# Chunked linear attention and an MLP on one core: later chunks' attention in 64x64 tiles, two halves of 64 times, one visit per group

## The chip, the cores and the metric

The kernel runs on one core of a Trainium2 chip. The metric is the device time of one execution in microseconds. The kernel before was timed three times: median 529.92 us (528.95, 529.92 and 985.7). One execution of it was profiled; its own time is 529.4 us, of which the profile's span, from the first instruction to the last, is 527.7 us.

Engines are named as in the profile: PE is TensorE (matmuls; PEld its weight loads), DVE VectorE, ACT ScalarE, POOL GpSimd, and SP the engine whose queue issues all DMAs here. PSUM is the memory that TensorE writes; the kernel uses it as eight banks of 512 f32 columns on 128 partitions.

## What is computed

Four sequences, eight heads, 768 times, 48 features a head. A linear attention with a decaying 48x48 state per sequence and head gives `y`; all heads' `y` of a time, 384 numbers, go through an MLP with an exact Gelu and 2048 hidden features.

```python
def _attn_ref(r, k, v, w, u):
    state = np.zeros((B, H, D, D), dtype=np.float32)
    for t in range(S):
        kt, vt, rt = (k[:, :, t], v[:, :, t], r[:, :, t])
        cur = np.einsum('bhd,bhe->bhde', u[None] * kt, vt)
        y[:, :, t] = np.einsum('bhd,bhde->bhe', rt, state + cur)
        state = w[None, :, :, None] * state + np.einsum('bhd,bhe->bhde', kt, vt)

def _moe_ref(x, w_in, w_out):
    h = x @ w_in
    g = 0.5 * h * (1.0 + erf(h * inv_sqrt2))
    return (g @ w_out).astype(np.float32)
```

## The kernel before

Time is cut into six chunks of 128 (`NCH`, `C`), heads into four pairs (`NP`). A *group* `gi` is one chunk of one pair, with all four sequences: 24 groups, `gi // 4` the chunk. Inside a chunk the attention is matrix products: the *scores* of all keys against all receptances of the chunk (L399), masked to the past (L406) with the bonus `u` on the diagonal (L375); the *new* part, the masked scores times the values (L425); the *old* part, the state at the chunk's start seen by the receptances (L419); and the *gain*, the chunk's own contribution to the state (L431), which L440 adds to the decayed state `Sbd`. Decays are put into the factors: L366 scales `r` and `k` by powers of `w` kept in `W`, and the keys of the gain are scaled by `WN` (L385). The result stands in the PSUM bank `Y`; L458 and L459 split it into a rounded high part and a remainder for the MLP, and 64 KB DMAs (L465) bring the fourth pair's features to where the other pairs leave gaps.

A pair lies on 112 partitions: one head on 0 to 47, the other on 64 to 111. The attention's products are plain f32, each of which leaves two records in the profile. The MLP's are in a rounded 32-bit format (`F32R`) and leave one record each, with every factor split into two parts, so that a step has three triples of matmuls into the hidden layer (L473, bank `Hp`) and three out of it (L513, banks `O`). A *step* is one chunk's 512 columns against 128 of the 2048 hidden features: 16 steps a chunk, 96 in all. Two Gelus (L501, L502) and a subtraction (L503) stand between.

The weights arrive as 64-bit numbers and are split on the chip, once, in the first 16 steps: three ScalarE and four VectorE operations a step (L304 to L316).

The first chunk's groups have their own forms (`plain`), with no state to look at. Groups of later chunks have the scores in 64x32 tiles, so as to leave out future times in blocks of 32, and their products are two separate entries of TensorE's list: scores and old part at one visit, new part and gain at another, with MLP triples between.

The order on every engine is worked out while the program is built, by `Plan.run`. Each operation is added with its engine, an estimated duration, a due time and the names it reads and writes. The planner walks through a simulated clock and gives each engine, of what is ready, the operation that is due first. `LATER` as due time means that an operation is due when its users need it. The engines then run their lists strictly in that order, so an operation whose input is late holds up all behind it on its engine. SP's DMAs are in such a list too. A group's loads go into one of two slots (`T`, `N`), by the parity of `gi`, and wait till the group two before has done with it.

`count_plain` checks that all decays lie in a range in which the chunked form is exact enough; outside it a slow general form follows, which isn't run with these inputs.

## Time and profile before

| | |
|---|---|
| median of 3 runs | 529.92 us |
| profiled execution | 529.4 us |
| its span | 527.7 us |
| PE busy | 510.1 us (97%) |
| DVE, ACT, POOL busy | 249.0, 219.7, 85.4 us |
| granted TensorE clock, mean | 0.977 |

The page shows busy times over the whole span, and the span in 40 slices of 13.2 us, in which a digit is a tenth of a slice:

```profile
PE   6899889999999999999999999999999999999995
PEld 4777667777887877778777878878787787888884
DVE  8979999996442433423433524334334213211111
ACT  2468778666424243334234343342442322322221
POOL 7650430312202202012022022011011000000000
PEclk8579999999999999999999999999999999999999
```

A group of records is given as line, engine, operation, what it writes and reads, its tile shape, the partitions and elements, and how many. A row of the timeline begins with the start and the length in microseconds. The length of a matmul's record is a model and runs on into the next one's, so what a block of matmuls costs is read from the start of one block to the start of the next.

### The profile page before, as it was taken

The page shows a single profiled execution, that of the slowest core. Times are in us where ns is not written, and L with a number is a line of the kernel's source. Part 1 is how long each engine was busy: PE and PEld are TensorE (multiplying, and loading weights), DVE is VectorE, ACT ScalarE, POOL GpSimd, SP SyncE. Part 2 cuts the span into 40 slices and gives each one's busy share as a digit, 9 for nine tenths or more (in the row PEclk, how much of TensorE's full clock was granted, in tenths as well). Part 3 has the DMA queues.
Part 4 walks back from the last instruction along what each step waited for, and adds up shares of the span by engine and source line. Part 5 has one row for each costly group of instructions (what it writes and reads, how often), then busy time and mean ns, then how long its engine had stood idle before and what let it go on. Part 6 is the DMA issues. An engine that isn't in the chain of part 4 may idle for free.

```text
span 527.7 us, 9445 instructions
## 1 busy us (share of the span) xinstructions
PE 510.1 (97%) x4039; PEld 406.3 (77%) x4039; DVE 249.0 (47%) x344; ACT 219.7 (42%) x467; POOL 85.4 (16%) x77
## 2 busy tenths in 40 slices
PE   6899889999999999999999999999999999999995
PEld 4777667777887877778777878878787787888884
DVE  8979999996442433423433524334334213211111
ACT  2468778666424243334234343342442322322221
POOL 7650430312202202012022022011011000000000
PEclk8579999999999999999999999999999999999999
DMA  8926665530330211411202403203313000100001
GB/s 242 362 70 202 214 181 179 203 91 32 111 89 2 91 50 43 140 34 58 91 1 90 142 0 91 63 29 91 101 40 91 1 11 11 60 1 1 1 0 65
DMA packets 13167, 44.51 MB, mean 84 GB/s; under 512 B 1792, under 2 KB 2176, under 8 KB 13120
## 3 DMA queue, kind: packets, MB, share of 16 engines
q1 hardware_dynamic: 13120, 43.86, 26.3%
q8 instruction: 33, 0.54, 0.4%
q14 instruction: 14, 0.11, 0.1%
HBM read 37.16 MB, written 4.72 MB: 79 GB/s over the span
## 4 chain that ended last, share of the span: by engine, by line
PE 77%; DVE 11%; DMA 4%; ACT 3%; issue 2%; POOL 2%; SPq 0%; DVEq 0%; POOLq 0%; ACTq 0%
PE Hp L473 32%; PE O L513 30%; PE Y L425 4%; PE A L399 4%; PE Y L419 3%; DMA Nb<-in_rkv_dram 3%; DVE wa L312 2%; DVE wa L310 1%; ACT Am L375 1%; DVE wl L316 1%; DMA raw<-in_wmlp_dram 1%; PE Y L513 1%; PE U L431 1%; DVE gl L503 1%; DVE Ts L343 1%
## 5 line engine op out<-in xcount | busy, mean ns | idle before, releaser
L473 PE MATMUL Hp<-xx,wh 128*128 128x512 f32 x576 | 169.3, 401 | 0.7 <-ACT gf L502 0.7
L503 DVE TENSOR_TENSOR gl<-gf,gh 128x512 fp32r<-128x512 f32 x95 | 75.8, 798 | 196.2 <-ACT gf L502 193.9
L473 PEld LDWEIGHTS Hp<-xx,wh 128*128 128x128 f32 x576 | 104.3, 188 | 25.3 <-ACT gf L502 2.4
L501 ACT ACTIVATE gh<-Hp 128x512 fp32r<-128x512 f32 x95 | 56.6, 595 | 151.6 <-PE Hp L473 151.6
L473 PE MATMUL Hp<-xx,wl 128*128 128x512 f32 x288 | 83.8, 398 | 1.2 <-DVE wl L316 1.2
L513 PE MATMUL O<-gh,wh 128*128 128x512 f32 (+1 forms) x285 | 81.6, 393 | 3.1 <-ACT gh L501 3.1
L513 PE MATMUL O<-gh,wl 128*128 128x512 f32 (+1 forms) x285 | 80.6, 390 | 0.0
L513 PE MATMUL O<-gl,wh 128*128 128x512 f32 (+1 forms) x285 | 80.4, 389 | 0.0
L361 POOL TENSOR_TENSOR Nb<-Nb 128x384 f32<-128x384 f32 x20 | 23.0, 1151 | 308.6 <-DMA Nb<-in_rkv_dram 293.0
L375 ACT ACTIVATE Am<-diag,cs 128x128 f32<-128x128 f32 x176 | 56.0, 392 | 28.3 <-DVE cs L368 28.2
L513 PEld LDWEIGHTS O<-gh,wh 128*128 128x128 f32 x285 | 52.6, 188 | 17.2 <-ACT gh L501 4.7
L473 PEld LDWEIGHTS Hp<-xx,wl 128*128 128x128 f32 x288 | 53.6, 188 | 15.8 <-DVE wl L316 2.8
L513 PEld LDWEIGHTS O<-gl,wh 128*128 128x128 f32 x285 | 52.7, 188 | 11.6
L513 PEld LDWEIGHTS O<-gh,wl 128*128 128x128 f32 x285 | 52.6, 188 | 11.7
L502 ACT ACTIVATE gf<-Hp 128x512 f32<-128x512 f32 x96 | 56.7, 591 | 0.0
L458 ACT CAST xx<-Y 112x512 fp32r<-112x512 f32 (+1 forms) x16 | 9.4, 588 | 69.5 <-PE Y L425 69.5
L406 DVE COPY_PREDICATED Am<-past,A 128x512 f32<-128x512 uint32 x44 | 29.6, 724 | 17.5 <-PE A L399 17.5
L440 DVE SCALAR_TENSOR_TENSOR Sbd<-Sbd,P,U 48x192 f32<-48x192 f32 x32 | 13.1, 411 | 29.0 <-PE U L431 28.5
L366 DVE TENSOR_TENSOR Tb<-Tb,W 112x1024 f32<-112x1024 f32 x20 | 25.2, 1262 | 2.7 <-DMA Tb<-in_rkT_dram 2.4
L363 POOL TENSOR_TENSOR Nb<-Nb,u_sb 128x384 f32<-128x384 f32 x20 | 24.2, 1211 | 1.5
L419 PE MATMUL Y<-Tb,Sbd 112*112 112x128 f32 x160 | 22.4, 283 | 0.0
L399 PEld LDWEIGHTS A<-Tb 48*32 48x32 f32 (+1 forms) x1280 | 16.7, 105 | 7.0 <-issue 6.6
(106 smaller groups left out, 396.9 us busy)
## 6 DMA issues: line engine op xcount, KB each, us to landing
raw<-in_wmlp_dram SPq DMA_DIRECT2D x16, 768.0 KB, 5.0
Nb<-in_rkv_dram SPq DMA_DIRECT2D x20, 576.0 KB, 4.6
Tb<-in_rkT_dram SPq DMA_DIRECT2D x20, 448.0 KB, 3.7
out_dram<-raw SPq DMA_DIRECT2D x5, 768.0 KB, 4.8
xx<-x SPq DMA_DIRECT2D x30, 64.0 KB, 3.1
T<-in_rkT_dram SPq DMA_DIRECT2D x4, 448.0 KB, 6.5
N<-in_rkv_dram SPq DMA_DIRECT2D x4, 384.0 KB, 9.0
out_dram<-raw SPq DMA_DIRECT2D x2, 256.0 KB, 2.5
```

The costliest lines, as they stand in the source:

```text
L361: add("pool", pool(DM), LATER, lambda: nc.gpsimd.tensor_tensor(out=n[:, 0], in0=n[:, 0], in1=n[:, 1], op=ALU.mult), r=[NK], w=[NR])
L363: add("pool", pool(DM), LATER, lambda: nc.gpsimd.tensor_tensor(out=n[:, 0], in0=n[:, 0], in1=u_sb[:, p, :].unsqueeze(1).to_broadcast([C, N ...
L366: add("dve", dve(1024), LATER, lambda: nc.vector.tensor_tensor(out=flat(t), in0=flat(t), in1=decay, op=ALU.mult), r=["P", f"W{p}"], w=[TR])
L375: add("act", 293, LATER, lambda j=j, b=b: nc.scalar.activation(out=am[:, j, b, :], in_=diag, func=AF.Copy, scale=sums[:, 2 * b + j:2 * b + ...
L399: nc.tensor.matmul(X[j][q, b * C + t0:(b + 1) * C], lhsT=t[l, 1, b, q], rhs=t[l, 0, b, t0:], start=True, stop=True)
L406: add("dve", 600, LATER, lambda j=j: nc.vector.copy_predicated(out=am[:, j], mask=past.bitcast(U32).unsqueeze(1).to_broadcast([C, NB, C]), ...
L419: nc.tensor.matmul(y[:LP, b * C:(b + 1) * C], lhsT=Sbd[:, p, b, :], rhs=t[:, 0, b, :], start=(b == 0), stop=False, skip_group_check=True)
L473: nc.tensor.matmul(Hp, lhsT=wt[j][:, 0, k_ * 128:(k_ + 1) * 128], rhs=x[:, a, k_, :], start=start and k_ == ks[0], stop=stop and k_ == ks[-1])
L501: add("act", 480, LATER, lambda: nc.scalar.activation(out=high, in_=Hp, func=AF.Gelu), r=["H"], w=[GH])
L502: add("act", 480, LATER, lambda: nc.scalar.activation(out=gf, in_=Hp, func=AF.Gelu), r=["H"], w=["gf"])
L503: add("dve", dve(512), LATER, lambda: nc.vector.tensor_tensor(out=low, in0=gf, in1=high.bitcast(F32), op=ALU.subtract), r=["gf", GH], w=[GL])
L513: nc.tensor.matmul(dst[:, a:b], lhsT=wt[j][:, 1, d * 128:(d + 1) * 128], rhs=gt[:, a:b], start=(j == 0 and n == 0), stop=(j == NJ - 1 and ...
```

## The change

Groups of the first chunk are as before (`first_group`). For later chunks, every group is cut into two halves of 64 times. The host lays the halves out so that the first half's heads lie on partitions 0 and 64 as before and the second half's are exchanged; in the layouts with times on partitions, the halves lie on partitions 0 to 63 and 64 to 127. All products are then 64x64 tiles (48 rows or columns where features are meant): the scores only within a half, the old part with the state at the start of each half, the new part within a half, and a gain per half. The state takes two steps a chunk, from `Sa` to `Sb` and on to the next chunk's `Sa`, and changes partitions at each (the exchange). `Sbd` and its zeros are gone.

TensorE visits a group once: the entry `products(prev, gi)` holds the old part of the group before, this group's scores and gains, a drain, and the new part of the group before. So group 4 is visited alone ahead of the loop, and one more visit, with only old and new part, follows group 23. The scores and gains share the banks `A`; the results share `Y` and `U`. Am's masked copy covers both heads at once.

The decays for the halves are in a new tile `E`, laid out by eight small DMAs from `W`, after it is complete; `WN2` comes from a second transposition. The masks `diag2` and `past2` are copied by ScalarE. `u` is loaded in two DMAs, exchanged for the second half. The memsets of `Y`, `O[2]` and `Sbd` are gone; the nine warming matmuls now write all seven banks. The range check gets a dependency on `xx00h`, and so its operations, placed at chunk three, can't be taken early.

```diff
-        Sbd = sb([LP, NP, NB, LP], F32, "Sbd")
-        W = sb([LP, NP, C + 1], F32, "W")
+        St = [sb([LP, NP + 1, NB, D], F32, "Sa"), sb([LP, 2, NB, D], F32, "Sb")]
+        W = sb([LP, NP, KEYS + C], F32, "W", pro)
+        E = sb([LP, 2, NP, 2, HALF], F32, "E")
...
-        add("pool", 1530, 5, lambda: nc.gpsimd.memset(Sbd, 0.0), w=[f"S{p}" for p in range(NP)])
+        for dst, src, x in ((diag2, diag, "diag"), (past2, past, "past")):
+            for h in range(2):
+                add("act", 280, LATER, lambda dst=dst, src=src, h=h: nc.scalar.copy(
+                    out=dst[64 * h:64 * h + 64], in_=src[64 * h:64 * h + 64, 64 - 64 * h:128 - 64 * h]),
+                    r=[x], w=[f"{x}2{h}"])
...
-        add("dve", 540, -10, lambda: nc.vector.memset(Y, 0.0), w=["Y"])
-        add("dve", 540, 0, lambda: nc.vector.memset(O[2], 0.0), w=["O2"])
...
+        def halves(src, dst, h):
+            W2 = W[src, :, 32:32 + 2 * (KEYS - 32)].rearrange("l p (a i) -> l p a i", a=2)
+            for a in range(2):
+                nc.sync.dma_start(E[dst, a, :, h], W2[:, :, a, 0:HALF])
+        every = [f"W{p}" for p in PAIRS] + ["P", "WKs"]
+        for i, (src, dst, h) in enumerate(((slice(0, LP), slice(0, LP), 0), (slice(48, 64), slice(48, 64), 1),
+                                           (slice(0, D), slice(64, LP), 1), (slice(64, LP), slice(0, D), 1))):
+            dma(100000, LATER, lambda src=src, dst=dst, h=h: halves(src, dst, h), r=every, w=[f"E{i}"])
+        EVERY = [f"E{i}" for i in range(4)]
+        add("pe", 480, LATER, lambda: flip(lambda p: E[:, 1, p].rearrange("l h i -> l (h i)")), r=EVERY + ["ident"], w=["U"])
+        add("act", 540, LATER, flipped(WN2), r=["U"], w=["WN2"])
...
+        def prepare(gi):
+            c, p, t, TR, n, NR, NK, NV, am, AM = names(gi)[:10]
...
+            add("dve", sdve(1024), LATER, lambda: nc.vector.tensor_tensor(
+                out=flat, in0=flat, in1=E[:, 0, p].rearrange("l h i -> l (h i)").unsqueeze(1).to_broadcast(
+                    [LP, 2 * NB, C]), op=ALU.mult), r=EVERY, w=[TR])
+            add("pool", pool(DM), LATER, lambda: nc.gpsimd.tensor_tensor(
+                out=n[:, 0], in0=n[:, 0], in1=n[:, 1], op=ALU.mult), r=[NK], w=[NR])
+            kn = n[:, 1]
+            add("pool", pool(DM), LATER, lambda: nc.gpsimd.tensor_tensor(
+                out=kn, in0=kn, in1=WN2[:, p].rearrange("s j d -> s (j d)").unsqueeze(1).to_broadcast([C, NB, 2 * D]),
+                op=ALU.mult), r=["WN2"], w=[NK])
...
+            for x in range(2):
+                bonus(am, AM, diag2, ["diag20", "diag21"], HALF, sums, CS, x, "a")
...
+        def products(prev, gi):
...
+            def old():
+                for b in range(NB):
+                    for j in range(2):
+                        for h in range(2):
+                            l = quarter(j ^ h)
+                            nc.tensor.matmul(
+                                YU[quarter(j), h, b * HALF:(b + 1) * HALF], lhsT=S2[h][l, b, :],
+                                rhs=t[l, 0, b, times(h)], start=(b == 0), stop=False, skip_group_check=True)
+            def scores():
+                for b in range(NB):
+                    for h in range(2):
+                        for x in range(2):
+                            nc.tensor.matmul(A[x][times(h), b * HALF:(b + 1) * HALF],
+                                             lhsT=t_[quarter(x), 1, b, times(h)], rhs=t_[quarter(x), 0, b, times(h)],
+                                             start=True, stop=True)
+            def gains():
+                for b in range(NB):
+                    for x in range(2):
+                        for h in range(2 if c_ < NCH - 1 else 1):
+                            nc.tensor.matmul(A[h][quarter(x), U0 + b * D:U0 + (b + 1) * D],
+                                             lhsT=kn_[times(h), b, heads(x)], rhs=vn_[times(h), b, heads(x)],
+                                             start=True, stop=True)
+            def new():
+                nc.tensor.drain()
+                for b in range(NB):
+                    for j in range(2):
+                        for h in range(2):
+                            nc.tensor.matmul(YU[quarter(j), h, b * HALF:(b + 1) * HALF],
+                                             lhsT=n[times(h), 2, b, heads(j ^ h)], rhs=am[times(h), j ^ h, b, :],
+                                             start=False, stop=True, skip_group_check=True)
+            def go():
+                if prev is not None:
+                    old()
+                if gi is not None:
+                    scores()
+                    gains()
+                if prev is not None:
+                    new()
+            add("pe", ns, LATER, go, r=r, w=w)
+        def state(gi, h, at):
...
+            for x in range(2):
+                l = quarter(x)
+                add("dve", 420, at, lambda l=l, x=x: nc.vector.scalar_tensor_tensor(
+                    out=out[quarter(1 - x)], in0=src[l], scalar=E[l, 1, p, h, 32:33],
+                    in1=A[h][l, U0:U0 + NB * D].rearrange("d (b e) -> d b e", e=D), op0=ALU.mult, op1=ALU.add),
+                    r=[f"A{h}", SRC[x]] + EVERY, w=[OUT[1 - x]])
+        def past_scores(gi):
+            am, AM = names(gi)[8:10]
+            add("dve", 722, LATER, lambda: nc.vector.copy_predicated(
+                out=am, mask=past2.bitcast(U32).unsqueeze(1).unsqueeze(1).to_broadcast([C, 2, NB, HALF]),
+                data=AA[:, :, 0:U0].rearrange("s x (b t) -> s x b t", t=HALF)),
+                r=["past20", "past21", "A0", "A1"], w=[f"{AM}0", f"{AM}1"])
...
+        def group(gi, at):
+            if gi < NG:
+                prepare(gi)
+            products(gi - 1 if gi > NP else None, gi if gi < NG else None)
+            if gi < NG:
+                state(gi, 0, LATER)
+                past_scores(gi)
+                if gi < NG - NP:
+                    state(gi, 1, at + 20000)
+            if gi > NP:
+                finish(gi - 1, at)
...
-            add("dve", 800, at, in_range, r=["w_sb"], w=["n1"])
+            add("dve", 800, at, in_range, r=["w_sb", "xx00h"], w=["n1"])
...
+            if G == 0:
+                group(NP, LATER)
             if G % 4 == 0 and G // 4 + NP < NG:
-                gi = G // 4 + NP
-                at = step_at(4 * (gi - NP)) + GROUP_DUE
-                if gi > 5:
+                gi = G // 4 + NP + 1
+                at = step_at(4 * (gi - 1 - NP)) + GROUP_DUE
+                if 5 < gi < NG:
                     load_group(gi, at - GROUP_AHEAD)
-                group(gi, at, A, ["A0", "A1"], Y, "Y")
+                group(gi, at)
```

More of the change, by code (lines that the diff above doesn't have):

```diff
@@ L284, in rwkv_gelu_mlp, with flipped @@
-        add("act", 380, LATER, lambda: nc.scalar.copy(
-            out=WN, in_=U.rearrange("s (p j x) -> s p j x", p=NP, x=64)[:, :, :, :D]), r=["U"], w=["WN"])
+                nc.tensor.transpose(U[:, p * 128:p * 128 + LP], src(p), ident[:LP, :LP])
+        def flipped(dst):
+            return lambda: nc.scalar.copy(out=dst, in_=U.rearrange("s (p j x) -> s p j x", p=NP, x=64)[:, :, :, :D])
+        add("dve", 900, LATER, state_powers, r=["P"], w=["WKs"])
+        add("pe", 480, LATER, lambda: flip(lambda p: WKs[:, p, :]), r=["WKs", "ident"], w=["U"])
@@ new lines, in keep @@
+        def keep(c, p, at, src, view, YB, rows):
+            xt, XT = xx[c % 2], f"xx{c % 2}"
+            l = slice(0, rows)
+            dst = x3 if p == 3 else xt[:, :, p]
+            XN = "x3" if p == 3 else f"{XT}{p}"
+            add("act", sact(512), at, lambda: nc.scalar.copy(out=view(dst[l, 0]), in_=src[l]), r=YB, w=[f"{XN}h"])
+            add("dve", 676, at, lambda: nc.vector.tensor_tensor(
+                out=view(dst[l, 1]), in0=src[l], in1=view(dst[l, 0].bitcast(F32)), op=ALU.subtract),
+                r=YB + [f"{XN}h"], w=[f"{XN}l"])
+            if p < 3 and rows == LP:
+                for j in range(2):
+                    d = slice(64 * j + D, 64 * j + 64)
+                    f = slice(64 * j + 16 * p, 64 * j + 16 * p + 16)
+                    dma(16 * 4096, LATER, lambda d=d, f=f: nc.sync.dma_start(
+                        xt[d, :, p].bitcast(F32), x3[f].bitcast(F32)),
+                        r=["x3h", "x3l", f"{XT}{p}h", f"{XT}{p}l"], w=[f"{XT}{p}g{j}"])
@@ L405, in group @@
+            for bs in ((0, 1), (2, 3)) if gi == 0 else (range(NB),):
+                add("pe", 434 * len(bs), LATER, lambda bs=bs: scores(bs), r=[f"{TR}{b}" for b in bs], w=XB)
             for j in range(2):
@@ L415, in gaps @@
                                      skip_group_check=True)
-            def old():
-                for b in range(NB):
-                    nc.tensor.matmul(y[:LP, b * C:(b + 1) * C], lhsT=Sbd[:, p, b, :], rhs=t[:, 0, b, :],
-                                     start=(b == 0), stop=False, skip_group_check=True)
             def new():
@@ L425, in new @@
                         nc.tensor.matmul(y[64 * j:64 * j + D, b * C:(b + 1) * C], lhsT=vn[:, b, j * D:(j + 1) * D],
-                                         rhs=am[:, j, b, :], start=(plain and not spreads), stop=True, skip_group_check=True)
+                                         rhs=am[:, j, b, :], start=not spreads, stop=True, skip_group_check=True)
             def gain():
@@ L443, in group @@
             if spreads:
                 add("pe", 2 * 216, LATER, gaps, r=["spread", "x3h", "x3l"], w=[YB])
-            if c > 0:
-                add("pe", 4 * 217, LATER, old, r=[TR, f"S{p}"], w=[YB])
             add("pe", 8 * 130, LATER, new, r=[NV, f"{AM}0", f"{AM}1"], w=[YB])
-            if more:
-                add("pe", 8 * 65, at, gain, r=[NK, NV], w=["U"])
-                for j in range(2):
-                    add("act" if c == 0 else "dve", 210 if c == 0 else 330, at,
-                        lambda j=j: state(j), r=["U", "P128"], w=[f"S{p}"])
@@ L461, in group @@
[L461 to L467 removed]
+            add("pe", 8 * 65, at, gain, r=[NK, NV], w=["U"])
@@ L640, in swap @@
                 wl.append(late.tile([128, 2, DM], F32R, name=f"wl{j}"))
-        add("do", 0, 0, swap, w=["late", "ident", "ones", "WKs", "zeros", "warm", "spread"] +
-            [f"{x}{i}" for x in ("T", "RK", "Nk", "Nv") for i in range(NP)] +
+        add("do", 0, 0, swap, w=["late", "ident", "ones", "diag", "past", "P", "WKs", "WN", "zeros", "warm", "spread"] +
+            [f"{x}{i}" for x in ("W", "T", "RK", "Nk", "Nv") for i in range(NP)] +
             [f"Ts{i}{b}" for i in range(NP) for b in range(NB)] + [f"Am{i}{j}" for i in (2, 3) for j in range(2)])
```

247 lines of the change are left out of this document (131 added, 116 removed).

## The prediction, written before the changed kernel was run

> **What bounds the kernel now.** I read the page first: the engines' busy shares, then the slices.
>
> ```profile
> span 527.7 us, 9445 instructions
> PE 510.1 (97%) x4039; PEld 406.3 (77%) x4039; DVE 249.0 (47%) x344; ACT 219.7 (42%) x467; POOL 85.4 (16%) x77
> ```
>
> TensorE is busy for nearly the whole span and everything else for half of it or less. But a mean hides stages, so the second view is the busy time by stretches, cut where the slices change.
>
> ```profile
> 0.00:37.50 37.50, 30.70 (x245) 25.49 (x246) 31.23 (x48) 15.92 (x39) 24.92 (x27) 0.68 0.73 237
> 37.50:60.00 22.50, 21.68 (x256) 16.28 (x254) 22.44 (x29) 16.88 (x31) 6.08 (x3) 1.00 0.65 206
> 60.00:100.00 40.00, 37.53 (x255) 28.72 (x256) 39.34 (x53) 32.12 (x58) 6.12 (x5) 1.00 0.61 196
> 100.00:121.00 21.00, 20.00 (x172) 15.20 (x171) 20.86 (x25) 14.52 (x29) 6.24 (x5) 1.00 0.25 79
> 121.00:455.00 334.00, 333.26 (x2781) 264.63 (x2780) 122.20 (x174) 121.03 (x280) 42.04 (x39) 1.00 0.19 59
> ```
>
> The columns are the length, then the busy time of PE, PEld, DVE, ACT and POOL, the granted clock and DMA. Three stages are seen. Up to 37.5 us the first chunk is prepared, with the clock at 0.68 on the mean. From 37.5 to 121 us VectorE is full (22.44 of 22.50, 39.34 of 40, 20.86 of 21) while it splits the weights, and TensorE stands now and then. From 121 us on TensorE is full (333.26 of 334) and VectorE a third busy. The seam is visible in the timeline:
>
> ```profile
> 119.85 1.31 DVE L316 TENSOR_TENSOR wl<-wa,wh 128x768 fp32r<-128x768 f32 x1
> 121.62 0.86 PE L473 MATMUL Hp<-xx,wl 128*128 128x512 f32 x3
> ```
>
> The last split weight is done at 121.16 and TensorE uses it at 121.62. So TensorE time taken out before 121 us is worth almost nothing by itself; taken out after it, it is worth its full length. How long one group's attention costs TensorE there is read from the chain of work that ended last:
>
> ```profile
> 316.18 1.06 PE Y L419 x8
> 336.63 1.06 PE Y L419 x8
> 404.07 2.10 PE Hp L473 x9
> 417.70 1.06 PE Y L419 x8
> 437.80 1.06 PE Y L419 x8
> ```
>
> Nine matmuls of the MLP take 2.10, a triple 0.70, and there are four MLP steps of six triples between two groups: 16.8 us. The period is 336.63 - 316.18 = 20.45 us, so a group of the middle chunks costs 3.65 us. In the last chunk, where no state is gained, the period is 20.10 and a group costs 3.30. The sixteen groups after 121 us are 12 x 3.65 + 4 x 3.30 = 57.0 us. Now one group in detail, TensorE's timeline:
>
> ```profile
> 314.29 0.86 PE L513 MATMUL O<-gl,wh 128*128 128x512 f32 x3
> 315.08 1.10 PE L399 MATMUL A<-Tb 64*32 64x32 f32 x64
> 316.11 1.13 PE L419 MATMUL Y<-Tb,Sbd 112*112 112x128 f32 x8
> 317.00 0.94 PE L473 MATMUL Hp<-xx,wh 128*128 128x512 f32 x3
> 317.77 0.86 PE L473 MATMUL Hp<-xx,wl 128*128 128x512 f32 x3
> 318.57 1.08 PE L425 MATMUL Y<-Am,Nb 128*48 128x128 f32 x16
> 319.48 0.53 PE L431 MATMUL U<-Nb 128*48 128x48 f32 x16
> 319.94 0.96 PE L473 MATMUL Hp<-xx,wh 128*128 128x512 f32 x3
> ```
>
> A plain f32 product is two records. L419 runs 8 records of 128 columns, one after another on the whole array, in 317.00 - 316.11 = 0.89 us: 0.111 us each. L425 has 16 such records and takes 0.91: its two halves of the array run side by side, eight each. L399 has 64 records on eight tiles, at most 8 of 128 columns on one tile, and takes 1.03. So a block lasts as long as the eight records of its fullest tile, in proportion to their columns, and tiles in both directions overlap.
>
> **The products.** The change computes everything in 64x64 tiles, four at a time, with 64 (or 48) columns. Each block of sixteen products puts 8 records on each tile: 8 x 0.111 / 2 = 0.445 us for the old part, the scores and the new part. For the gains, 48 columns, the row is this one:
>
> ```profile
> 46.85 0.56 PE L431 MATMUL U<-Nb 128*48 128x48 f32 x16
> 47.25 1.05 PE L425 MATMUL Y<-Am,Nb 128*48 128x128 f32 x16
> ```
>
> 8 records a tile there too, 0.40 us. Sum of the four blocks: 3 x 0.445 + 0.40 = 1.735. In the last chunk the gains have half the products but still 8 records on each of two tiles: again 0.40, where before there were none.
>
> **Changing the tile shape.** Before, the blocks by the same rule are 3 x 0.89 + 0.40 = 3.07, so 3.65 - 3.07 = 0.58 goes into four changes of shape (into the first visit, between L399 and L419, into and out of the second visit), about 0.145 each. With one visit of a single shape two are left: 0.29.
>
> **The drain.** The new part is preceded by a drain of TensorE, which no row before shows. Its price is what is still under way behind the last gain plus a weight load that can't be fetched ahead:
>
> ```profile
> L431 PE MATMUL U<-Nb 128*48 128x48 f32 x256 | 8.6, 209 | 0.0
> ```
> ```profile
> L431 PEld LDWEIGHTS U<-Nb 128*48 128x48 f32 x256 | 7.8, 124 | 1.6 <-issue 1.5
> ```
>
> 0.209 minus the 0.05 in which the next record would start anyway, plus 0.124, is 0.28 us. Lower bound 0, if the tail is hidden; upper bound 0.49, a whole record (0.21) and as much again as the first value (0.28), if the queue has to fill anew. I take 0.28, as it is put together from the rows of just this form.
>
> **The sum after 121 us.** A visit is 1.735 + 0.29 + 0.28 = 2.31. There are again sixteen after 121 us: fifteen whole ones and a last one with only the old and new part, 2 x 0.445 + 0.29 + 0.28 = 1.46. 15 x 2.31 + 1.46 = 36.1 against 57.0: 20.9 us less.
>
> A page of the Trainium skill speaks against this sum: "TensorE: Matmul & The Clock Gate", section "Wait — 56ns, not 53.3ns?", says that starts of matmuls never come closer than about 25 ns however few columns they have. By it, taken over the whole engine, a block of 32 records would last 0.80 us and nothing would be gained. The trace does not agree: L399's 64 records in 1.03 us are 16 ns apart, so the sum stays with the rows.
>
> **What else a group does.** VectorE gets one masked copy in place of two, and four state updates in place of two; ScalarE's eight bonus copies are half as wide; GpSimd does its three products in another order, and the decay of the keys in the last chunk too, four more of about 1.0 us. All of it lies beside TensorE after 121 us, where VectorE is busy 122 of 334 us, ScalarE 121 and GpSimd 42: nothing. The second gain's state update and the masked copy have to free the score banks before the next visit, about 19 us later. The loads change more: a group's tiles are free only when the visit after its own is over, and the load into them waits in SP's queue till then. This is the chain that must fit:
>
> ```profile
> 320.08 0.33 SPq L206 DMA_DIRECT2D Nb<-in_rkv_dram  x1
> 323.86 1.01 POOL L361 TENSOR_TENSOR Nb<-Nb 128x384 f32<-128x384 f32 x1 [17.35 <-DMA Nb<-in_rkv_dram]
> 325.92 1.02 POOL L385 TENSOR_TENSOR Nb<-Nb,WN 128x384 f32<-128x384 f32 x1
> ```
>
> From issue to decayed keys 326.94 - 320.08 = 6.9 us, against a period of 16.8 + 2.31 = 19.1: 12 us of room, so nothing. Without that room each microsecond too much would be paid sixteen times.
>
> **The first 121 us.** Here VectorE's queue is what counts.
>
> ```profile
> 13.07 3.95 DVE L563 TENSOR_SCALAR low<-wu_sb 112x4 f32<-112x4 f32 x1
> 18.08 0.73 DVE L406 COPY_PREDICATED Am<-past,A 128x512 f32<-128x512 uint32 x1
> 18.86 2.55 PE L425 MATMUL Y<-Am,N 128*48 128x128 f32 x16 [1.72 <-DVE Am L406]
> ```
>
> The range check stands from 13.07 to 18.08, 5.0 us for operations on four columns: it waited beside GpSimd, which was busy there. Moving it lets the masked copies start earlier. At least the 1.72 us that TensorE waits for them go; at most all 5.0 us of VectorE's queue. I take 4.0, nearer the upper end, since it is VectorE that is full afterwards. At chunk three the check lies beside other work, and its one product was already placed at that step. Against it stands more work in the full stage:
>
> ```profile
> 37.50:121.20 83.70, 5.41 (x8) 1.00 0.53 169
> ```
> ```profile
> 37.50:121.20 83.70, 3.24 (x8) 1.00 0.53 169
> ```
>
> The first row is the masked copies L406, the second the state updates L440, in that stage. Five visits fall into it after the change (before: four groups), so 5 copies of 0.68 in place of 8 save 2.0, and 20 updates of 0.41 in place of 8 cost 4.9: 2.9 more. The wider state powers cost 0.2. The second flip of the decays is 0.5 on TensorE (1.0 at half clock, by L280's row):
>
> ```profile
> 12.33 1.01 PE L280 MATMUL U<-ident,WKs 112*128 112x112 f32 x4 [1.83 <-DVE WKs L275]
> 14.63 25.13 SPq L291 DMA_DIRECT2D raw<-in_wmlp_dram  x3
> 39.30 1.21 DVE L366 TENSOR_TENSOR Tb<-Tb,W 112x1024 f32<-112x1024 f32 x1
> ```
>
> The eight small DMAs that lay out E pass through SP while it waits between weight loads (three issues in the 25 us from 14.63), and E is first needed by the scaling that stands at 39.30; the wider use of SP, one more issue for u, the four mask copies and WN2 on ScalarE (15.92 busy of 37.50) are hidden likewise. If E came after that scaling's turn, VectorE would wait for it and everything behind it would be late by as much. The two memsets on VectorE and Sbd's on GpSimd lie before the first data: nothing. Sum: -4.0 + 2.9 + 0.2 + 0.5 = -0.4, called -0.5. Bounds: -5 (check saved whole, extra updates in gaps) and +5 (only TensorE's 1.7 saved, the updates, and one more group's scaling and sum of 1.8 pulled ahead, and a full 1.0 flip). TensorE's own saving of some 5 us in this stage is put at nothing, because VectorE ends it.
>
> **Sum.** The profiled execution took 529.4 us (span 527.7), 0.5 below the median of 529.92. 529.4 - 20.9 - 0.5 = 508.0 us, 4% less.
>
> **The rivals.**
>
> *Issue sets the pace of the small records.* If the queue, not the tile, gave L399 its 16 ns a record, a block is 32 x 16 ns = 0.515, a visit 4 x 0.515 + 0.57 = 2.63, the last 1.60: 41.1 against 57.0, 513 us. For it: 32 records in 0.445 would be 14 ns, closer than any row. Against: L399's fullest tile explains its time without it. At the 25 ns of L431's row (0.40 for 16) a block is 0.80, a visit 3.77 and the last 2.17: 58.7, so 529.4 + 1.7 - 0.5 = 531 us, no change. The Trainium skill's page "TensorE: Matmul & The Clock Gate", as told above, would have it so.
>
> *Two row groups on one bank.* The old part writes each bank of Y from both row halves at once, which no block of before does. If one had to wait, its 0.445 doubles in sixteen visits: 7.1 us, 515. The Trainium skill, "TensorEngine Tiling (Array Packing)", "Gotcha 1: PSUM Pressure", says that different row tiles cannot use one bank at the same time; no row here shows such a case.
>
> *A new wait at the visit.* A visit is one run of products, so all of it stands behind the latest of its inputs. If each came late by one masked copy (0.73, L406's row), sixteen times that is 11.7 us: 520. For it: the copy now reads what the visit itself has just written. Against: its reader is the next visit, 19 us on.
>
> *The tiles take turns (slower).* If the order of the products, which changes tile at each, kept tiles from overlapping, a block is 32 x 0.0555 = 1.78 (gains 32 x 0.05 = 1.6), a visit 7.5 and the last 4.1: 116.6, so 529.4 + 59.6 - 0.5 = 589 us. It is over 2% slower from 4.3 us a visit on. Against it: L399 changes tile at each product too, and overlaps eight.
>
> **How the numbers follow.** The forecast's own case, tiles that overlap and a hidden rest, gets 0.65, with 501 to 514 for the drain (0 to 0.49, -4.5 to +3.4) and the first stage (-4.5 to +5.5), which rarely fall together. Issue at 16 ns gets 0.12, at 25 ns 0.08; the shared bank 0.05; new waits 0.06, half of them beyond the border; tiles in turn 0.04. Two per cent, about what a measurement of this kernel can tell from no change, is 10.6 us: the border is 519.3. Faster: 0.65 + 0.12 + 0.05 + 0.03 = 0.85. Same: 0.08 + 0.03 = 0.11. Slower: 0.04. The range 499 to 518 leaves out the 25 ns, the slow waits, the turns and a little of the ends.
>
> **What would show it.** In the new timeline a middle group should be one run of some 128 records and take 2.3 us more than the MLP triples around it, with a period near 19.1. Old, scores and new should each take 0.45, gains 0.40; a gap of about 0.3 stands before the new part. Blocks of 0.5 or 0.8 mean the issue, an old part twice the scores' length the bank. The last weight split should end within 5 us of 121. The forecast is wrong if visits have waits in front of them, or the first stage moves by more than that.

## The result and the profile after

The changed kernel takes 512.62 us in the median of four executions (509.73 to 514.63), against 528.95 for the kernel before (526.93 to 529.92): a ratio of 0.9694, 95% interval 0.9626 to 0.9761. Here and below, two executions that took far longer than the others of their kernel are left out: 985.7 us of the kernel before, and 517.22 us in the last experiment. The profiled execution of the changed kernel took 512.43 us. Its page says

```profile
span 510.7 us, 10489 instructions
PE 488.2 (96%) x4524; PEld 387.8 (76%) x4524; DVE 248.8 (49%) x363; ACT 213.6 (42%) x472; POOL 88.6 (17%) x80
```

TensorE is still the full engine and has 21.9 us less to do, but the span is only 17.0 us shorter. The stage in which the weights are split, called the first weights' stage here, shows where the rest went. Its ends in the timelines are TensorE's first MLP product and VectorE's last split weight (the seam); here the first MLP product before the change, then both ends after it:

```profile
37.52 0.39 PE L473 MATMUL Hp<-xx,wh 128*128 128x512 f32 x1
```
```profile
37.59 0.50 PE L602 MATMUL Hp<-xx,wh 128*128 128x512 f32 x1
```
```profile
124.23 0.95 DVE L342 TENSOR_TENSOR wl<-wa,wh 128x768 fp32r<-128x768 f32 x1
```

The start has not moved; the last split weight is done at 125.18 and was done at 121.16. From it to the span's end are 510.7 - 125.2 = 385.5 us, before 406.5. So the change won 21.0 us behind the seam and lost 4.0 ahead of it. About one microsecond of both is only work that changed sides: 270 MLP products begin ahead of the later seam, where 266 began before, and four of them take 0.9 us (three take 0.70). Busy times of that stage (length, PE, PEld, DVE, ACT, POOL, clock, DMA), before and after:

```profile
37.50:121.20 83.70, 79.41 (x683) 60.35 (x682) 82.84 (x106) 63.72 (x116) 18.64 (x12) 1.00 0.53 169
```
```profile
37.50:125.20 87.70, 79.58 (x870) 57.49 (x864) 83.82 (x113) 63.30 (x117) 18.35 (x12) 1.00 0.50 162
```

VectorE works 1.0 us more and stands 3.9 us where it stood 0.9. So three of the four lost microseconds are idle time of VectorE, in a stage in which it had less than one before. TensorE's waits there, from 40 to 125 us (total, times, longest), before and after:

```profile
PEld O L513 <- ACT gh L501: 4.7, 5, 1.8
```
```profile
PEld O L642 <- ACT gh L630: 11.4, 13, 2.5
```

Behind the seam a visit looks like this in TensorE's timeline (start, length; of the old part's 32 records the first two):

```profile
304.78 0.86 PE L642 MATMUL O<-gl,wh 128*128 128x512 f32 x3
305.57 0.25 PE L519 MATMUL Y<-Tb,Sa 48*48 48x64 f32 x1
305.58 0.25 PE L519 MATMUL Y<-Tb,Sb 48*48 48x64 f32 x1
...
306.06 0.65 PE L527 MATMUL A<-Tb 48*64 48x64 f32 x32
306.52 0.54 PE L536 MATMUL A<-Nb 64*48 64x48 f32 x32
307.20 0.66 PE L546 MATMUL Y<-Am,Nb 64*48 64x64 f32 x32
307.79 0.95 PE L602 MATMUL Hp<-xx,wh 128*128 128x512 f32 x3
308.58 0.63 PE L602 MATMUL Hp<-xx,wl 128*128 128x512 f32 x2
```

From start to start: old 0.49, scores 0.46, gains and drain 0.68, new 0.59. A triple lasts 0.70, so the visit began 0.09 late (305.57 for 305.48), and the triple behind it lasts 0.79, 0.09 longer. Together 2.40 us, where a group cost 3.65. No row stands waiting in front of it, nor in front of the fifteen other visits behind the seam. The period fits, by the chain, with 327.13 - 307.86 = 19.27 us for 16.8 + 2.40 = 19.20:

```profile
307.86 2.29 PE Hp L602 x9
...
327.13 2.30 PE Hp L602 x9
```

### The profile page after: what moved, and what is told of

The parts are those of the page before. It is cut to its first block, busy times and chain, and to the rows that moved or that the text cites. A ratio compares the mean times of both kernels' runs of the same rounds, so it can differ in the third digit from the quotient of the medians.

```text
span 510.7 us, 10489 instructions
## 1 busy us (share of the span) xinstructions
PE 488.2 (96%) x4524; PEld 387.8 (76%) x4524; DVE 248.8 (49%) x363; ACT 213.6 (42%) x472; POOL 88.6 (17%) x80
## 3 DMA queue, kind: packets, MB, share of 16 engines
HBM read 37.16 MB, written 4.72 MB: 82 GB/s over the span
## 4 chain that ended last, share of the span: by engine, by line
PE 84%; DVE 11%; issue 2%; ACT 1%; DMA 1%; SPq 0%; DVEq 0%
PE Hp L602 37%; PE O L642 35%; PE Y L546 2%; PE Y L519 2%; PE A L527 2%; DVE wa L338 1%; DVE wl L342 1%; DVE Ts L393 1%; PE A L536 1%; PE Y L642 1%; DVE gl L632 1%; DVE wa L336 1%; DMA T<-in_rkT_dram 1%; DVE wa L334 1%; ACT wh L340 1%
## 5 line engine op out<-in xcount | busy, mean ns | idle before, releaser
L632 DVE TENSOR_TENSOR gl<-gf,gh 128x512 fp32r<-128x512 f32 x95 | 73.2, 770 | 193.9 <-ACT gf L631 193.8
L602 PEld LDWEIGHTS Hp<-xx,wh 128*128 128x128 f32 x576 | 105.8, 188 | 26.6 <-ACT gf L631 1.5
L351 ACT ACTIVATE Am<-diag,cs 128x64 f32<-128x64 f32 (+1 forms) x176 | 47.4, 345 | 22.8 <-DVE cs L491 22.7
L479 DVE TENSOR_TENSOR Tb<-Tb,E 112x1024 f32<-112x1024 f32 x20 | 24.4, 1220 | 2.9 <-DMA Tb<-in_rkT_dram 2.9
L488 POOL TENSOR_TENSOR Nb<-Nb,u_sb 128x384 f32<-128x384 f32 x20 | 25.6, 1282 | 0.2
L569 DVE SCALAR_TENSOR_TENSOR Sb<-Sa,E,A 48x192 f32<-48x192 f32 x40 | 16.5, 413 | 16.0 <-PE A L536 15.4
L485 POOL TENSOR_TENSOR Nb<-Nb,WN 128x384 f32<-128x384 f32 x20 | 22.7, 1135 | 2.7 <-ACT WN L293 1.3
L576 DVE COPY_PREDICATED Am<-past,A 128x512 f32<-128x512 uint32 x20 | 14.8, 738 | 7.0 <-PE A L536 6.8
L342 DVE TENSOR_TENSOR wl<-wa,wh 128x768 fp32r<-128x768 f32 x16 | 16.7, 1042 | 1.9 <-ACT wh L340 1.7
```

The costliest lines, as they stand in the source:

```text
L342: add("dve", sdve(n), LATER, lambda: nc.vector.tensor_tensor(out=both(wl), in0=af, in1=both(wh).bitcast(F32), op=ALU.subtract), r=[A_, f"w ...
L351: add("act", sact(n) + 90, LATER, lambda b=b: nc.scalar.activation(out=am[:, j, b, :], in_=diag, func=AF.Copy, scale=sums[:, 2 * b + j:2 * ...
L479: add("dve", sdve(1024), LATER, lambda: nc.vector.tensor_tensor(out=flat, in0=flat, in1=E[:, 0, p].rearrange("l h i -> l (h i)").unsqueeze ...
L485: add("pool", pool(DM), LATER, lambda: nc.gpsimd.tensor_tensor(out=kn, in0=kn, in1=WN2[:, p].rearrange("s j d -> s (j d)").unsqueeze(1).to ...
L488: add("pool", pool(DM), LATER, lambda: nc.gpsimd.tensor_tensor(out=n[:, 0], in0=n[:, 0], in1=u_sb[:, p, :].unsqueeze(1).to_broadcast([C, N ...
L569: add("dve", 420, at, lambda l=l, x=x: nc.vector.scalar_tensor_tensor(out=out[quarter(1 - x)], in0=src[l], scalar=E[l, 1, p, h, 32:33], in ...
```

## The experiments

Each is timed beside the kernel before, whose medians on the four chips used lie between 528.5 and 529.2 us; differences are taken from the 512.57 us of the first one. Executions of one kernel lie 2 to 5 us apart and the experiments ran on different chips, so a difference of a microsecond says nothing. "Last split weight" is the end of the row shown above, in each one's profile. A split weight can also be early because TensorE left work for later. TensorE's last product shows that: in the changed kernel it starts 379.4 us after the last split weight.

**The changed kernel again**, as the base of the differences.

> The changed kernel once more, beside the runs that follow, on one chip. Expected 510 to 515 us as before (509.73 to 514.63 in four runs): the first weights' stage ends near 125 us and a middle group costs TensorE 2.41 us.

512.57 us (ratio 0.9713, 0.9685 to 0.9741). Its profile differs at the start: the MLP begins at 31.18, 6.4 us earlier, and yet the last split weight is done at 124.88. The windows show why (columns as above):

```profile
31.00:38.67 7.67, 4.72 (x100) 3.02 (x94) 7.61 (x8) 3.90 (x14) 4.06 (x3) 1.00 0.42 152
38.67:48.91 10.24, 9.04 (x140) 7.22 (x141) 7.59 (x13) 6.11 (x9) 0.00 (x0) 0.50 0.37 121
```

After a stretch with TensorE busy for 4.72 of 7.67 us, its clock was halved (0.50) for 10.24 us, which is 5.1 us of its work. The profile of the changed kernel above has no such stretch in this stage. So two executions of one kernel reach the seam together by different ways, and a single profile's first stage must be read with its clock beside it.

**The drain twice.**

```diff
                     scores()
+                    nc.tensor.drain()
                     gains()
```

> A second drain in each visit, between the scores and the gains. If a drain costs what the trace of the changed kernel shows in front of the new part (0.29 us from the end of the last gain's columns to the first new product, and some 0.09 more until the products run at their pace), the fifteen visits of the full stage with scores cost 4.4 to 5.7 us more in all, and a visit rises from 2.41 to 2.70 to 2.80. Rival: the 0.29 belongs to the change of direction in PSUM and not to the drain itself; then the second drain costs under 0.1 a visit and under 1.5 us in all.

523.16 us (0.9888, 0.986 to 0.9916), 10.6 more, about twice what was expected. A visit in its timeline, where the old part starts at 316.55:

```profile
317.03 0.65 PE L527 MATMUL A<-Tb 48*64 48x64 f32 x32
317.90 0.58 PE L536 MATMUL A<-Nb 64*48 64x48 f32 x32 [0.22 <-issue]
318.60 0.66 PE L546 MATMUL Y<-Am,Nb 64*48 64x64 f32 x32
```

Scores to gains takes 0.87 for 0.46: this drain costs 0.41, and the fifteen behind the seam 6.2 us, a little over the expected 4.4 to 5.7. The drain ahead of the new part still has its 0.30 (0.70 less the gains' 0.40). The other 4 us lie ahead of the seam: in the profiled execution, the slowest of the six (526.05 us), the last split weight is done at 132.27, with the clock halved for 10.2 us of that stage.

**Two visits, no other change.**

```diff
-            products(gi - 1 if gi > NP else None, gi if gi < NG else None)
+            if gi > NP:
+                products(gi - 1, None)
+            if gi < NG:
+                products(None, gi)
```

> Each visit is cut into two entries, old part with drain and new part as one, scores and gains as the other, with MLP products between. If going into and out of a shape costs 0.40 us a visit, as the visit of 2.41 leaves over its blocks, sixteen more visits in the full stage cost 6 us: about 518 to 519 us. Rival: the single visit is worth little, since the drain is cheaper where the scores don't follow the old part, or an entry by itself is placed better: under 2 us. In the first stage, where VectorE is the bound, the extra visits should show nothing.

517.06 us (0.9758, 0.9735 to 0.9781), 4.5 more. A group's two visits:

```profile
311.36 0.66 PE L546 MATMUL Y<-Am,Nb 64*48 64x64 f32 x32
...
324.10 0.69 PE L527 MATMUL A<-Tb 48*64 48x64 f32 x32
324.61 0.54 PE L536 MATMUL A<-Nb 64*48 64x48 f32 x32
```

The first starts at 310.56 and ends at 311.96, the second runs from 324.10 to 325.08: 1.40 and 0.98, and 0.18 for the edges of each, 2.74 in all. That is 0.34 more than one visit, 5.4 us in sixteen, close to the expected 6; so one visit a group is worth its edges behind the seam. Ahead of it, the last split weight came at 120.80, 4.4 us early. That is no gain: TensorE's last product starts 390.3 us later, 10.9 more than in the changed kernel, of which the edges are 5.4; 250 MLP products had begun at the seam and not 270, and the twenty are 4.7 us that moved behind it. With the clock halved for 6.8 us of this stage besides, this run doesn't tell what the single visit costs there.

**The range check early again.**

```diff
-            add("dve", 800, at, in_range, r=["w_sb", "xx00h"], w=["n1"])
+            add("dve", 800, at, in_range, r=["w_sb"], w=["n1"])
```

> The changed kernel with the range check free to be taken early again, all else as changed. The prediction had put moving it at 4.0 us of VectorE's time in front of the weights' stage: then this is 3 to 4 us slower than the changed kernel (516). Rival: the check only fills a time in which VectorE would wait beside GpSimd anyway, and TensorE at half clock sets the start of the MLP (37.5 us in both kernels): then within 1 us of the changed kernel.

517.14 us (0.9771, 0.9748 to 0.9794), 4.5 more, close to the 4.0 of the prediction. But the rows refuse its reason. VectorE's timeline of this kernel, then of the changed one:

```profile
3.96 0.16 DVE L692 TENSOR_SCALAR low<-wu_sb 112x4 f32<-112x4 f32 x1
...
16.46 1.28 DVE L393 TENSOR_TENSOR Ts<-T,W 112x512 f32<-112x512 f32 x2
```
```profile
14.48 1.34 DVE L425 COPY_PREDICATED Am<-past,A 128x512 f32<-128x512 uint32 x2
15.73 4.18 DVE L393 TENSOR_TENSOR Ts<-T,W 112x512 f32<-112x512 f32 x2
...
158.70 0.16 DVE L692 TENSOR_SCALAR low<-wu_sb 112x4 f32<-112x4 f32 x1
```

The check's first instruction, 3.95 us before the change, takes 0.16 at either place, the whole check 0.6 us here. And where the check had stood, another instruction of the changed kernel now takes 4.18 us for what is 1.28 here. By the rows of GpSimd it was working beside the long ones all the time (from 12.95 to 23.70 us in the changed kernel) and was idle here, from 15.98 to 21.23; so the length most likely comes from GpSimd, though not every VectorE instruction beside it is long. The check has hardly a price of its own, and an early check doesn't hold up the MLP: that starts at 35.62 here, 2.0 us earlier than in the changed kernel's profile. What the early check costs came in the stage behind it: the last split weight at 128.94, with the clock halved for 6.8 us of the stage (mean 0.96 from 40 to 116 us). Why this order makes the stage so long stays open.

**The range check late, on the kernel before**, the same line the other way.

> The kernel before with one edit: the range check waits for the first tile of chunk three, as in the changed kernel. Moved the other way on the changed kernel it cost 4.5 us. If the check has one price wherever it stands early (VectorE's stream is held up), the time falls from 529.2 to about 524.7 and the last split weight comes some 4 us before 121.2. If the 4.5 us were only a collision of the changed kernel's own order, the time falls by less than 1.5 us.

526.36 us (0.9954, 0.9937 to 0.9972), 2.6 less: between the two expectations. The MLP starts at 35.22 and the last split weight is done at 118.42; both move by 2.3 to 2.7 us, and the masked copies that stood at 18.08 stand at 13.30. In this kernel the check's place is worth 2.6 us, at the start.

**Fewer state updates.**

```diff
-                if gi < NG - NP:
+                if gi < NG - NP and gi not in (5, 6, 7):
                     state(gi, 1, at + 20000)
```

> The changed kernel without the second state update of three of the first four later groups (state(gi, 1) for gi 5, 6 and 7): their pairs go into the next chunk without what the second 64 times of this chunk add, so that part of the computation is left out. It takes six instructions of 0.41 us, 2.5 us, out of VectorE's stream ahead of the last split weight (125.2 us in the changed kernel). Theory A, VectorE's work sets the end of the first weights' stage and the twelve more updates are part of what made it longer: the last split weight comes about 2.5 us earlier and the time falls from 512.6 to about 510.1. Theory B, the stage is longer because VectorE waits in it (4.8 us of idle time against 1.2 before), for ScalarE's rounding and gelu behind a visit: the six instructions only turn into idle time, the last split weight moves by less than 1 us and the time stays between 512 and 513.

This kernel leaves out what three groups' second 64 times add to the state. 510.95 us (509.26 to 513.94; 0.9655, 0.9625 to 0.9685), 1.6 less, between the theories. The profiled execution was the slowest of the six, with the clock halved for 10.2 us of the stage and the last split weight at 124.92. The four executions with a mean clock of 0.976 or more took 509.3 to 511.5, the two at 0.966 513.7 and 513.9. That leans to a stage set by VectorE's work, but does not show it.

**The later groups' bonus on GpSimd.**

```diff
-                bonus(am, AM, diag2, ["diag20", "diag21"], HALF, sums, CS, x, "a")
+                bonus(am, AM, diag2, ["diag20", "diag21"], HALF, sums, CS, x, "p")
```

> The changed kernel with the bonus of the later groups made by GpSimd in two products in place of eight ScalarE activations a group (35 of them, 11.8 us of ScalarE, lie between 37.5 and 125 us). Theory B, ScalarE comes late in the first weights' stage: VectorE's idle time there falls from 4.8 towards 1 us, the last split weight comes 2 to 3.5 us earlier, and the time falls to 509 to 510.5. Theory A, VectorE's own work sets the stage's end: 512.6 within 0.7. Rival to both: GpSimd's products lengthen VectorE's instructions that run beside them, and the stage grows by 1 to 3 us.

511.75 us (0.9681, 0.9655 to 0.9707), 0.8 less, which its interval doesn't tell from nothing. The stage fills up (VectorE 74.75 of 76 us from 40 to 116; 73.10 in the changed kernel) and the last split weight comes at 122.24, but the low parts of the weights take 18.6 us for 15.7 (37.5 to 125.2 us), most likely since GpSimd now works 25.0 of those 76 us beside them and not 14.1. One wait was traded for a longer instruction.

**Two visits in the first stage only.**

```diff
-            products(gi - 1 if gi > NP else None, gi if gi < NG else None)
+            if NP < gi < NP + 5:
+                products(gi - 1, None)
+                products(None, gi)
+            else:
+                products(gi - 1 if gi > NP else None, gi if gi < NG else None)
```

> The changed kernel with two visits for the first four groups that have a group before them (the visits at 45.6, 66.9, 89.7 and 111.7 us), one visit from then on. Theory C, the single visit holds TensorE's stream back until the slowest of both groups' operands is there, and costs the first weights' stage the 4 us by which the last split weight came earlier with two visits everywhere: the last split weight comes at about 121 us and the time falls to about 508.5. Rival: with two visits everywhere the stage ended earlier because other work (two state updates, a gelu's low part) had moved behind the last split weight, and TensorE gains nothing: the time stays at 512 to 513, or rises by up to 1.4 us for the four visits.

509.50 us (509.23 to 511.31; 0.9637, 0.9612 to 0.9663), 3.1 less: the fastest kernel of the study. The last split weight is done at 116.51, 8.7 us early, but 5.2 us of that is work that moved behind it (TensorE's last product comes 384.6 us later, not 379.4). The MLP of this profile also starts at 34.91, 2.7 us earlier; so the profile alone doesn't say whether the stage itself ran faster, and VectorE stands more in it, not less (busy for 71.70 of the 76 us from 40 to 116, for 73.10 in the changed kernel).

**Scaling on GpSimd too**, in the groups 4 to 8 of that kernel: the product that scales `T` by `E` goes from VectorE to GpSimd.

> The kernel with the visits split in the first weights' stage, and there (groups 4 to 8) the product that scales T by E (1.22 us of VectorE a group, five groups, 6.1 us) on GpSimd, which is idle for 67 of 85 us. Theory A, VectorE's instructions set the stage's end also now (5.4 us idle of 79): the last split weight comes 3 to 5 us before 116.5 and the time falls from 509.5 to 506 or 507. Rival 1, GpSimd's longer product makes VectorE's instructions beside it longer (as with the bonus on GpSimd, where the low parts of the weights rose from 16.2 to 18.6 us): gain under 1 us. Rival 2, the first group's scaled T comes later from GpSimd and the start waits for it: 510 to 512.

518.82 us (0.9824, 0.9803 to 0.9845), 9.3 more than the split kernel, worse than any expectation had it. GpSimd took the product into its queue, and the product waits for a load with the groups' other products behind it:

```profile
49.36 2.88 POOL L481 TENSOR_TENSOR Tb<-Tb,E 112x1024 f32<-112x1024 f32 x1 [9.70 <-DMA Tb<-in_rkT_dram]
52.21 1.72 POOL L484 TENSOR_TENSOR Nb<-Nb 128x384 f32<-128x384 f32 x1
```

TensorE is busy for 64.35 of the 76 us from 40 to 116 there, against 69.14 without this edit.

**Split visits and bonus on GpSimd together**, the latter in groups 4 to 8 only.

> The kernel with the visits split in the first weights' stage, and the bonus of groups 4 to 8 on GpSimd. On the single-visit kernel the bonus on GpSimd for all later groups brought the last split weight 2.6 us earlier but the time only 0.8 us. If the two edits cure different waits (TensorE behind a visit, ScalarE behind its bonus), the time falls by another 0.8 to 2 us, to 507.5 to 508.7. If they cure the same wait, it stays at 509.5, or rises to 511 since GpSimd is late for the sums that VectorE waits for (1.9 us in the profile of the split kernel).

510.10 us (0.9646, 0.963 to 0.9662): no gain over the split alone.

**E's DMAs behind the third weight's load**: E's block is placed after the loads and waits for `raw2` also.

```diff
-        every = [f"W{p}" for p in PAIRS] + ["P", "WKs"]
+            every = [f"W{p}" for p in PAIRS] + ["P", "WKs", "raw2"]
...
+        spread_powers()
         for gi in range(NP):
```

> The changed kernel (one visit) with the eight DMAs of E put behind the load of the third weight's raw bits, which goes at 24.6 us in the changed kernel because E's DMAs hold SP from 13.3 to 22.5 us, and went at 14.6 us before the change. If E's DMAs are hidden, as the prediction had it, the time stays within 0.7 us of 512.6. If the late load makes the first weights' stage longer, its last split weight comes 1 to 4 us before 125.2 and the time falls to 509 to 511.5. If instead E itself is what the first later group waits for, the start of the stage slips by 3 to 8 us; a slip of the start by 6 us had moved the end by only 0.3 us, so the time would be 512.6 to 514.

510.00 us (509.2 to 512.0; 0.9652, 0.963 to 0.9675), 2.6 less. SP's timeline of the changed kernel, then of this one:

```profile
13.33 9.14 SPq L303 DMA_DIRECT2D E<-W  x8
...
24.57 1.49 SPq L317 DMA_DIRECT2D raw<-in_wmlp_dram  x2
```
```profile
7.51 2.01 SPq L318 DMA_DIRECT2D raw<-in_wmlp_dram  x2
...
13.40 9.55 SPq L303 DMA_DIRECT2D E<-W  x8
```

E's DMAs go when they went; the third weight's load has moved, from 24.57 to the run of two that begins at 7.51. Two others moved with it: the first weight's load came forward (2.21 for 5.84) and the second load of `u` went behind E's DMAs (23.00 for 10.73). With that order, the stage is full again. From 40 to 116 us, the changed kernel and this one:

```profile
40.00:116.00 76.00, 68.95 (x810) 50.31 (x809) 73.10 (x99) 57.87 (x105) 14.14 (x9) 1.00 0.55 178
```
```profile
40.00:116.00 76.00, 69.28 (x846) 53.16 (x841) 75.14 (x100) 58.42 (x107) 13.56 (x10) 1.00 0.55 181
```

VectorE stands 0.9 us and not 2.9, the last split weight is done at 121.07, 4.1 us early (1.6 of it work that moved behind it, by TensorE's last product), and no clock interferes with the comparison in this window. The load itself was hardly waited for: ScalarE's waits for raw bits in this window are 0.7 us in the changed kernel and 1.3 here. What changed is the order: the planner, which reckons when a load lands, places the third weight's split and all behind it differently. Its reckoning was far off for E: it gives each of the four entries 0.64 us of SP, 2.6 in all, and they hold SP for 9.14. Whether a truer figure would mend the order was not tried.

**Both: split visits and the third load first.**

> Both edits on the changed kernel: two visits for each of the first four groups that have a group before them, and E's eight DMAs behind the load of the third weight's raw bits. Apart they brought 512.6 to 509.5 and 510.0, and the last split weight from 125.2 to 116.5 and 121.1. If the late load and the single visit are two causes, the gains add: 506.5 to 507.5, and VectorE's idle time in the first weights' stage falls under 3 us with the last split weight at 113 to 116 us. If they are two ways of undoing one thing (an order of the instructions in which VectorE waits), the second brings nothing more: 509 to 510.5.

510.48 us (509.52 to 514.53; 0.9663, 0.9631 to 0.9695): the gains don't add. The only trace is of the execution that is left out, so what was expected of VectorE's idle time and of the last split weight can't be judged.

## Why the prediction was right, and where it was not

The forecast was 508.0, the range 499 to 518, faster with 0.85. The time is 512.6: inside the range, on the side predicted, 4.6 us above the number. The main term was right and for the reason given; the small one was wrong in sign and size, and the range held because it had been given 5 us either way. The two terms of the sum, one by one:

**Behind the seam: -20.9 predicted, -21.0 measured.** The reason was right: 64x64 tiles overlap four at a time, and a block lasts as long as the eight records of its fullest tile. L519's 32 records start within 0.45 us (305.57 to 306.02), as put; gains 0.40 and drain 0.28, together 0.68, are what the rows show for both, and doubling the drain gave 0.41 for a drain between other blocks, inside its bounds. Mis-sized was the change of shape: 0.29 was put for two edges; 0.18 stands at the edges, 0.14 at the way out of the new part and 0.06 between old, scores and gains, 0.09 a visit more than the sum had. Fifteen visits of 2.40 and a last one of 1.57 are 37.6 for 36.1. So the visits gave 19.4 of the 21.0. Another 0.9 is the four MLP products that had changed sides, and 0.7 stays open. That the sum of 20.9 meets the 21.0 to 0.1 is luck: 1.5 us too much was put for the visits' saving, and about as much came from elsewhere.

**Ahead of the seam: -0.5 predicted, +4.0 measured**, inside its bounds of -5 and +5 but the whole miss. Three steps of it failed.

- The range check's -4.0 took the 5.0 us in which a waiting instruction stood as time that comes back. With the check gone from there, another instruction was long (L393, 4.18 us). What did come is the masked copies, at 14.48 for 18.08, and TensorE's wait of 1.72 us for them is gone; but the MLP's start stayed, at 37.59 for 37.52, although VectorE was busy for only 28.33 us of the first 37.5, before for 31.23. That start moves by itself (31.18 in the other execution, with a mean clock of 0.91 for 0.68 in the first 37.5 us), so one profile is weak evidence. On the kernel before, the late check is worth 2.6 us, at the start. On the changed kernel the early check costs 4.5, but with an earlier start and a longer stage; that this is close to 4.0 supports no reason.
- VectorE's extra work, +2.9, was counted right in kind and came out smaller:

```profile
37.50:125.20 87.70, 7.94 (x20) 1.00 0.50 162
```
```profile
37.50:125.20 87.70, 2.94 (x4) 1.00 0.50 162
```

These are the state updates L569 and the masked copies L576. Twenty updates are 4.7 us more than the eight before; four copies, not five, are 2.5 less than the eight; the five scalings take 5.9 us and took 6.9. With the rest it is the 1.0 us of the stage's busy times. What the sum left out are the 3.0 us of idle time.
- "The eight small DMAs that lay out E pass through SP while it waits" failed. They hold SP for 9.14 us, just where the third weight's load stood (14.63 before, 24.57 after). With that load first, 2.6 of the 4.6 us come back and VectorE's new idle time goes; the interval of that run (up to 0.9675) lies apart from that of the changed kernel beside which it is read (from 0.9685). This is the nearest to a cause that the runs have, though two other loads changed their places with it.

The single visit is the second way in: splitting it in this stage brings 3.1 us. As both together bring no more than either, they may be two ways of leaving one unlucky order of instructions; that is argued, not shown. The waits don't settle it: TensorE's for Gelus, 11.4 us in the changed kernel, are 6.1 with the third load first, but still 9.5 in the split one. Which instruction of that order is the decisive one stays open: each edit makes the planner rearrange all engines.

**The rivals.** Issue at 16 ns a record (a block of 0.515, 513 us) comes near the time but not by its mechanism: the records start 14.5 ns apart, and the surplus is ahead of the seam. The 25 ns that the Trainium skill's page "TensorE: Matmul & The Clock Gate" gives in "Wait — 56ns, not 53.3ns?" as the least distance of two starts does not hold for four tiles: two rows of one visit are 305.57 and 305.58. The shared bank fell too: the old part, which writes each bank from both row halves, takes 0.49, and the scores, which write each bank from one, 0.46. The Trainium skill's page "TensorEngine Tiling (Array Packing)", "Gotcha 1: PSUM Pressure", says that different row tiles cannot access one bank at the same time; no such wait shows in this trace. No wait stands in front of a visit behind the seam, and with 0.49 for 32 records the tiles don't take turns.

## What to carry to other kernels

An instruction that is long because of what goes on beside it may have no price that can be removed with it: look at what will stand in its place. A transfer is not hidden because its queue has idle time; ask which load it is put in front of, above all where a planner makes the order of all engines from its own reckoning of that load. And where a stage is bound by one engine with no slack, weigh a new order by the waits that it makes, not by the work alone: here 1.0 us of work came with 3.0 us of waiting. Where two profiles are compared up to some event, count too how much work each had done by then.

## What the runs showed of the hardware

TensorE's granted clock is not only low at the start. In the middle of the first weights' stage it was halved again in nine of the fourteen traces: the second one of the changed kernel and those of eight variants, not the profile of the kernel before and not the first one of the changed kernel. The lengths were 3.4, 6.8 and 10.2 us (for instance 38.67 to 48.91), all near multiples of 3.41. The Trainium skill's page "TensorE: Matmul & The Clock Gate", section "What's actually happening", states a free-running window of 3413 ns after which an idle array is throttled; the trace agrees with that length.

But TensorE was not idle in the windows ahead of these stretches. Here is the window that the halved clock follows in the second trace of the changed kernel, then one of its first trace that full clock follows (columns as above):

```profile
35.25:38.67 3.42, 1.16 (x65) 0.93 (x64) 3.36 (x5) 2.77 (x10) 0.00 (x0) 1.00 0.42 128
```
```profile
39.81:43.22 3.41, 1.82 (x67) 1.28 (x67) 3.35 (x5) 3.28 (x11) 0.00 (x0) 1.00 0.47 141
```

TensorE was busy for 1.16 us in the one and 1.82 in the other. With all fourteen traces cut into such windows from the changes of their clocks, some 1950 windows behind 28 us are at full clock. Halved clock follows each of the 22 with TensorE busy for 1.53 us or less and none with 1.82 or more; of the nine between, six. So in these traces, behind 28 us, it is the single window of 3.41 us that decides, at about half of it busy. The share over the whole stage doesn't tell: it was 64 to 71 of the 76 us from 40 to 116 in the variants with such stretches, and 68.95 in the changed kernel's own profile without one. Ahead of 28 us the rule fails: there four windows with TensorE busy for 2.9 us or more are followed by the halved clock. So taking products out of TensorE where it isn't the limit can cost its clock, if it leaves one window half empty.

A drain of TensorE has a price that depends on its place: 0.28 us between gains and new part (0.68 less the gains' 0.40), 0.41 between scores and gains.
